# First batch of a sparse attention and feed-forward kernel: one score task for a pair of heads, over two accumulation banks, with the heads crosswise in the second

## The chip, the cores and the metric

The kernel runs on one core of a Trainium2 chip. The metric is the device time of one execution in microseconds (us): 869.84 us, the median of three runs (869.70 to 870.52). One more execution was taken with the hardware profiler; every duration below is from it.

The core has five engines with an instruction queue each, which run their queues in order. TensorE (PE) multiplies matrices into the banks of its accumulation memory; VectorE (DVE), ScalarE (ACT) and GpSimd (POOL) do elementwise work; SyncE (SP) issues transfers from memory. POOL does not read the accumulation banks here. An engine waits for another through semaphores.

## The reference

```python
def _attn_ref(q, k, v):
    scores = scale * np.matmul(q, k.transpose(0, 1, 3, 2))      # 8 batches, 8 heads, 576 x 576
    rel = pos[:, None] - pos[None, :]
    mask_local = (rel >= 0) & (rel < 32)
    mask_strided = (rel >= 0) & (pos[None, :] % 32 == pos[:, None] % 32)
    # heads 0 to 3 local, heads 4 to 7 strided
    scores = np.where(masks, scores, -1e9)
    attn = softmax(scores)                                       # (sum + 1e-9)
    return np.matmul(attn, v)

def _moe_ref(x, w_in, w_out):                                    # 4608 tokens, 512 -> 2048 -> 512
    h = x @ w_in
    g = np.maximum(h, 0.0) + np.log1p(np.exp(-np.abs(h)))
    return g @ w_out
```

## The kernel before, in words

Attention touches only a band of the scores: 32 queries see 64 keys. Heads go in pairs; a pair's 576 queries are 18 blocks of 32 queries by 64 keys, put as nine *chunks* of 128 rows by 64 columns: row 64 x place + 32 x head + lane, where place is 0 or 1. The feed-forward part takes chunks of 512 tokens: 16 steps `hidden` (twelve 128x512 products, line 819) and 16 steps `output` (twelve more, line 860) for each chunk. Each fp32 number is split into a high and a low part, so weights and activations need some preparation on ACT, DVE and POOL.

The batches after the first run their attention inside the dense stream of products, ordered by a planner. The change is about what stands before that stream: batch 0, four pairs n = 0 to 3 (0 and 2 local, 1 and 3 strided). Its order is a list written out by hand, `FIRST` (line 44): every name is a task, and each engine gets its instructions in that order. `ON_POOL`, `ON_VECTOR` and `WIDE` say which engine or which form a task takes. The names, n a pair and j a part of it:

- `q`, `k`, `v`, `wi`, `wo`: transfers, issued by SP; `W` and `W15` and the like: products on zeros that keep PE active.
- `S` scores (line 414). Before, a pair has two: part 0 has chunks 0 to 5, part 1 chunks 6 to 8 (`SPLIT`, line 25), each in a bank of its own, py[2 (n mod 2) + part]. The mask is added by products too: `ident_b` picks the rows (line 422). Pairs 0 and 2 use the same two banks, 1 and 3 the other two.
- `X` row maxima (line 575, DVE), `x` their negative as a bias (line 579, DVE or POOL), `E` exponentials (ACT). `E` takes one instruction with its accumulator for each chunk (line 585), or, for a part named in `WIDE`, one instruction for the whole part (line 567) after a subtraction `Y` on DVE (line 562), and then sums `Z` on DVE (line 571). `E` without `Y` reads the bank; with `Y`, the bank is free after `Y`.
- `r`, `R`, `M`: guard (622), reciprocal (626), normalization (630).
- `T` three transposes on PE (line 693) into one of two free banks, `C` the copy out of it (ACT or DVE), `V` the product with v (line 712).
- `H` and `L`: high and low part of the attention output for the feed-forward part (lines 753 and 751).
- `a`, `B`, `d`, `h`, `l` with `i` or `o` and a number: the five steps that prepare a block of weights.
- `Fa0`, `F0`, `Fa1`, `F3`, ...: `hidden` of chunk 0 (`Fa` the first three quarters of it); `O0`, ...: `output`. `D4` and `J4` are the q layout and the scores of the first pair of batch 1, `Y40` takes the mask and frees `J4`'s bank.

`late_scores` (line 457), for later batches, holds the same form of products as `S`: 64x32 weights, 64 columns. It writes two banks in turn, and puts the two heads crosswise in the second one.

Of the kernel before, what the change touches and what calls it, by code (L numbers as in the profile page):

```python
# [45 lines left out]
x10 r0 wi3 v2 E10 x11 E11 Bi0 R0 wi2 ao0 M0 W15 S20 X20 T01 S21 di0 x20 E20 v3 S30 wo1 S31 hi0 r1
T00 C01 ai1 Bo0 R1 X21 Y21 k4 q4 X30 wi4 X31 E21 li0 Y30 C00 T02 Z21 wi6 x31 M1 V00 do0 r2 C02 Bi1
E30 E31 T11 wi9 V02 R2 Z30 V01 H00 M2 C11 L00 wo2 T10 T12 H01 C10 C12 L01 T21 V10 r3 ai3 wo3 R3 M3
ho0 Bi3 V12 lo0 C21 V11 H10 L10 T22 H11 wi12 L11 T20 C20 wi8 C22 ai2 V21 V20 V22 T30 H20 T31 W23 W17
di1 C30 di3 wo6 L20 Bi2 H21 L21 di2 T32 hi3 hi2 V30 C31 C32 V31 hi1 ao1 V32 Bo1 Km li3 Fa0 H30 L30  # L50
H31 L31 D4 li2 v4 do1 J4 li1 Y40 ai4 F0 ho1 Bi4 ai6 A0 Ae0 q5 Fa1 F1 wi10 Al0 Y42 Y41 ai9 X4 di4 lo1
u0 s4 hi4 Gh0 wi14 A1 Bi9 E4 Bi6 Gl0 F3 Ae1 Al1 O0 di6 di9 hi6 ao3 u1 Kz Kl F2 li4 A3 wo15 ao2 k5
Bo3 wo13 Ae3 li6 ao6 wo4 wi5 hi9 Gh1 Al3 Gl1 li9 Z4 ai8 u3 Bi8 Bo6 r4 di8 F6 wi7 wo8 A2 Bo2 Ae2 do2
R4 Al2 O1 M4 do3 u2 W18 wo11 hi8 Gh3 ho3 ho2 Gh2 D5 Gl3 A6 Ae6 wo9 do6 ho6 wo5 Gl2 P43 lo2 wo7 F4
P40 P42 Al6 A4 ai5 Ae4 lo3 u6 Al4 ai7 P41 u4 li8 Bi7 q6 ai10 lo6 Gh4 Bi5 O2 Gh6 J5 di5 Y50 wo10 hi5
di7 ao4 li5 Bo4 O3 Y51 X5 hi7 li7 Bi10 s5 F5 do4 E5 wi11 ho4 di10 Gl4 v5 k6 Z5 F9 H41 Gl6 ao7 H40 A5
Bo7 ao5 Ae5 A9 Al5 lo4 r5 Bo5 ao9 R5 M5 do5 L40 wi15 Ae9 O4 u5 Al9 wo14 L41 do7 F7 ho5 Gh5 u9 ho7
P52 Gl5 lo5 A7 hi10 Ae7 P53 Gh9 P50 Al7 u7 F8 lo7 Gl9 ai12 wi13 D6 ai11 O5 P51 Gh7 Bo9 Bi11 di11 J6
Y60 O6 Bi12 do9 A8 Y62 Y61 hi11 li10 ho9 ao8 X6 Bo8 di12 s6 Ae8 hi12 E6 li11 F10 do8 Gl7 O7 Al8 li12
v6 Z6 u8 r6 ho8 A10 R6 M6 lo8 Gh8 ai13 Ae10 P61 Al10 Gl8 F11 A11 u10 k7 ao10 wo12 Bi13 Ae11 F12 di13  # L60
ai14 lo9 Gh10 W19 O8 hi13 ao11 Gl10 P62 Al11 H50 li13 ai15 P60 u11 A12 Bo10 F13 Ae12 Gh11 q7 k8 D7
O9 Bi14 H51 Bi15 Al12 Gl11 Bo11 di14 hi14 P63 A13 L51 Ae13 do10 L50 u12 Al13 u13 ho10 lo10 ao12 W21
do11 J7 ho11 di15 Bo12 Y71 H61 O10 H60 li14 hi15 li15 lo11 ao15 Gh13 do12 v7 Gh12 q8 F14 ho12 Y70
ao13 X7 Gl12 Gl13 Bo13 F15 s7 do13 E7 O11 A14 Z7 L60 r7 Ae14 ho13 Al14 R7 lo12 A15 u14 L61 M7 Ae15
# [1177 lines left out]
```

## Time and profile before

| | us |
|---|---|
| median of three runs | 869.84 |
| profiled execution, its own time | 871.17 |
| its span in the trace | 869.4 |
| PE busy in the span | 860.9 |
| DVE, ACT, POOL busy | 595.6, 411.6, 97.4 |

The span runs from the first to the last instruction of the program. PE busy counts every product from its start to its modelled end, so that 99% busy is not 99% of PE's peak; what helps the reader is where PE is not busy, and what it does where it is busy without doing dense products.

### The profile page before, as it was taken

What the parts mean: (1) busy time and instruction counts of PE and PEld (TensorE: products, weight loads), DVE (VectorE), ACT (ScalarE), POOL (GpSimd) and SP (SyncE); (2) the same over time, 40 slices, a digit from 0 to 9 for tenths busy, and PEclk for the clock granted to TensorE, in tenths of its full rate; (3) what the DMA queues carried; (4) which work ended last, traced back from release to release, by engine and by line L of the source; (5) the groups of instructions that cost most, each with busy time, mean ns of one, the idle gap of its engine ahead of it and who ended that gap; (6) DMA issues with size and microseconds to landing.
All of it is one profiled execution on the core that took longest, in us unless ns stands there. A gap on an engine that the chain in (4) does not pass through costs nothing.

```text
span 869.4 us, 15756 instructions
## 1 busy us (share of the span) xinstructions
PE 860.9 (99%) x6312; PEld 704.8 (81%) x6312; DVE 595.6 (69%) x1283; ACT 411.6 (47%) x730; POOL 97.4 (11%) x117
## 2 busy tenths in 40 slices
PE   8999999999999999999999999999999999999998
PEld 5788888888888888888888888888888888888886
DVE  4999968777777787777777787777877433333332
ACT  6887745444444454444544444435344343334333
POOL 4667532121200000000000000000000000000000
PEclk9999999999999999999999999999999999999999
DMA  9983112111301121011301131112100010001001
GB/s 320 377 309 124 43 29 89 44 56 30 104 29 37 34 85 48 15 56 29 104 29 56 29 104 29 35 35 81 54 15 16 1 48 1 1 1 49 1 1 48
DMA packets 46462, 56.41 MB, mean 65 GB/s; under 512 B 3322, under 2 KB 31670, under 8 KB 46390
## 3 DMA queue, kind: packets, MB, share of 16 engines
q1 hardware_dynamic: 46102, 55.09, 19.6%
q8 instruction: 49, 0.80, 0.4%
q10 hardware_dynamic: 288, 0.33, 0.1%
q14 instruction: 23, 0.19, 0.1%
HBM read 45.97 MB, written 9.44 MB: 64 GB/s over the span
## 4 chain that ended last, share of the span: by engine, by line
PE 98%; DVE 1%; ACT 1%; issue 0%; POOL 0%; DVEq 0%; ACTq 0%; POOLq 0%
PE py L860 45%; PE ph L819 45%; PE ps L538 1%; PE ph L485 1%; PE ps L524 1%; PE ph L469 1%; PE py L440 1%; PE pv L712 1%; PE idle L883 1%; PE ph L693 0%; PE po L524 0%; PE py L422 0%; PE po L538 0%; POOL w_o L295 0%; ACT x_h L753 0%
## 5 line engine op out<-in xcount | busy, mean ns | idle before, releaser
L860 PE MATMUL py<-w_o,gh 128*128 128x512 f32 x1152 | 358.0, 392 | 0.0
L819 PE MATMUL ph<-x_h,w_i 128*128 128x512 f32 x1152 | 355.4, 390 | 0.4 <-POOL w_o L295 0.2
L819 PEld LDWEIGHTS ph<-x_h,w_i 128*128 128x128 f32 x1152 | 215.7, 188 | 46.5 <-DVE u L840 1.0
L860 PEld LDWEIGHTS py<-w_o,gh 128*128 128x128 f32 x1152 | 214.1, 188 | 45.4
L831 ACT ACTIVATE u<-ph 128x512 f32<-128x512 f32 x144 | 86.2, 598 | 321.9 <-PE ph L819 321.9
L840 DVE SCALAR_TENSOR_TENSOR u<-ph,u 128x512 f32<-128x512 f32 x144 | 99.3, 689 | 191.1 <-ACT u L836 190.3
L860 PE MATMUL py<-w_o,gl 128*128 128x512 f32 x576 | 224.2, 389 | 0.0
L819 PE MATMUL ph<-x_l,w_i 128*128 128x512 f32 x576 | 224.1, 389 | 0.0
L860 PEld LDWEIGHTS py<-w_o,gl 128*128 128x128 f32 x576 | 108.1, 188 | 22.9
L819 PEld LDWEIGHTS ph<-x_l,w_i 128*128 128x128 f32 x576 | 108.1, 188 | 22.6
L836 ACT ACTIVATE u<-u 128x512 f32<-128x512 f32 x144 | 91.0, 632 | 4.3
L834 ACT ACTIVATE u<-u 128x512 f32<-128x512 f32 x144 | 91.0, 632 | 4.3
L853 DVE TENSOR_TENSOR gl<-u,gh 128x512 fp32r<-128x512 f32 x118 | 81.8, 695 | 9.8
L667 DVE STREAM_TRANSPOSE masks_pt<-kT_prob 32x128 f32<-32x128 f32 (+2 forms) x220 | 63.4, 288 | 2.8
L295 DVE CAST gh<-u 128x512 fp32r<-128x512 f32 x129 | 57.5, 446 | 10.0 <-DVE u L840 0.5
L614 ACT ACTIVATE kT_prob<-kT_prob 128x594 f32<-128x594 f32 (+2 forms) x28 | 22.1, 788 | 52.6 <-DVE kT_prob L608 52.6
L853 POOL TENSOR_TENSOR gl<-u,gh 128x512 fp32r<-128x512 f32 x26 | 35.7, 1374 | 76.7 <-DVE gh L295 66.2
L646 DVE STREAM_TRANSPOSE pt_groups<-kT_prob 32x160 f32<-32x160 f32 (+1 forms) x112 | 39.6, 354 | 3.1
L646 DVE STREAM_TRANSPOSE masks_pt<-kT_prob 32x160 f32<-32x160 f32 (+1 forms) x112 | 39.6, 353 | 3.0
L618 DVE TENSOR_REDUCE st<-kT_prob 128x11 f32<-128x594 f32 (+2 forms) x28 | 24.6, 879 | 20.5 <-ACT kT_prob L614 20.5
L295 ACT COPY qT<-kT_prob 128x576 f32<-128x576 f32 x28 | 35.7, 1275 | 2.3 <-DMA kT_prob<-in_qk_dram 1.3
L753 ACT CAST x_h<-ps 128x288 fp32r<-128x288 f32 (+5 forms) x34 | 12.0, 372 | 42.2 <-PE ps L524 22.3
(117 smaller groups left out, 603.9 us busy)
## 6 DMA issues: line engine op xcount, KB each, us to landing
kT_prob<-in_qk_dram SPq DMA_DIRECT2D x42, 288.0 KB, 3.8
out_dram<-o SPq DMA_DIRECT2D x35, 256.0 KB, 3.6
ri<-in_moe_w_in_dram SPq DMA_DIRECT2D x16, 512.0 KB, 7.3
ro<-in_moe_w_out_dram SPq DMA_DIRECT2D x16, 512.0 KB, 8.9
kT<-in_qk_dram SPq DMA_DIRECT2D x14, 288.0 KB, 6.6
v_in<-in_v_dram SPq DMA_DIRECT2D x14, 162.0 KB
v_in<-in_v_dram SPq DMA_DIRECT2D x14, 160.0 KB, 3.3
v_in<-in_v_dram SPq DMA_DIRECT2D x14, 128.0 KB, 3.1
```

The lines of the kernel that those rows point to most:

```text
L295: (engine.copy if engine is nc.scalar else engine.tensor_copy)(dst, src)
L614: nc.scalar.activation(pv, pv, AF.Exp, scale=SCALE)
L618: nc.vector.tensor_reduce(sm, pv, axis=AX.X, op=ALU.add)
L646: nc.vector.transpose(dst[:, :, :32], src[:, :, :32])
L667: nc.vector.transpose(pt_late[lo : lo + 32, h, first : first + src.shape[1], col : col + 32], src,)
L819: nc.tensor.matmul(ph, lhsT=w32["i", f][:, half, cc * P : (cc + 1) * P], rhs=x_of(x, cc)[:, t0 : t0 + n], start=(i == 0), stop=(i == 3 * N ...
L831: nc.scalar.activation(us[c, f], phs[c, f], AF.Abs)
L834: nc.scalar.activation(u, u, AF.Exp, scale=-1.0)
L836: nc.scalar.activation(u, u, AF.Ln, bias=1.0)
L840: nc.vector.scalar_tensor_tensor(u, in0=phs.pop((c, f)), scalar=0.0, in1=u, op0=ALU.max, op1=ALU.add)
L853: engine.tensor_tensor(g, us.pop((c, f)), ghs[c, f].bitcast(F32), op=ALU.subtract)
L860: nc.tensor.matmul(py[t], lhsT=g[:, sl], rhs=w32["o", f][:, half], start=(f == 0 and n == 0), stop=(f == NFC - 1 and n == 2),)
```

## The change

A pair's scores become one task `S{n}` that fills both of its banks. `SPLIT` is now five and four chunks. The chunks are issued in the order 0, 5, 1, 6, 2, 7, 3, 8, 4, so that the two banks take turns, and in the second bank head 0 stands in the rows of head 1 and the other way round. The masks are added by products of 64 rows by 32 columns of weights, one for each place and head (8 for a local pair, 12 for a strided one, where the second bank needs two pieces of the mask; before, 4 of 128 rows by 64 columns). For that the mask comes twice into a region of `qT`, once in each half of the partitions, by two transfers from ACT's queue; the old copy `mask_b` comes later by SP's queue (`mk`). A second identity `flip` with the halves exchanged, made by two copies on ACT, takes the transposed heads of the second bank back to their places.

`FIRST` and the three lists are written anew: part 0 of pair 0 and both parts of pair 3 are `WIDE` (before: part 1 of pair 2 and part 0 of pair 3), and other casts and copies are on other engines.

```diff
-SPLIT = [(0, 6), (6, 9)]
+SPLIT = [(0, 5), (5, 9)]
 FIRST = """
-mask k0 q0 k1 W S01 q1 wi0 S00 q2 k3 X01 x01 k2 X00 S11 E01 wo0 ai0 x00 S10 q3 wi1 E00 X11 X10 v0 v1
+mask q0 W k0 S0 X00 X01 x01 wi0 q1 ai0 Y00 Bi0 E00 k1 di0 E01 k2 q2 S1 X11 wo0 Z00 x11 X10 S2 r0 R0
...
 WIDE = """
-21 30
+00 31 30
...
+    mask_early = qT[:, : 6 * 64].bitcast(BF16)
...
+    flip = room[2][:, 2 * NTILE * D + P : 2 * NTILE * D + 2 * P]
+    for h in range(2):
+        nc.scalar.copy(
+            flip.rearrange("p (a h c) -> p a h c", a=2, h=2)[:, :, h],
+            ident_b.rearrange("p (a h c) -> p a h c", a=2, h=2)[:, :, 1 - h],
+        )
...
+    def mask_pieces(n, part):
+        lo, hi = SPLIT[part]
         if is_local(n):
-            return mask_b[:, : 6 * 64] if part == 0 else mask_b[:, 64 : 4 * 64]
-        return mask_b[:, 6 * 64 :] if part == 0 else mask_b[:, 6 * 64 : 9 * 64]
+            return [(lo, hi, part, None)]
+        if part == 0:
+            return [(lo, hi, 6, 0)]
+        return [(lo, 6, 6 + lo, 0), (6, hi, 6, 1)]
...
-            for place in range(2):
-                nc.tensor.matmul(
-                    ps[rows[place], : 64 * (hi - lo)],
-                    lhsT=ident_b[:, rows[place if is_local(n) else part]],
-                    rhs=mask_of(n, part),
...
+            for part in range(2):
+                pieces = mask_pieces(n, part)
+                for lo, hi, chunk, sort in pieces:
+                    for place in range(2):
+                        for h in range(2):
+                            to = 64 * place + 32 * (h if part == 0 else 1 - h)
+                            head = slice(64 * h, 64 * h + 64)
+                            one = 64 * h + 32 * (place if sort is None else sort)
+                            at = 64 * (lo - SPLIT[part][0])
+                            nc.tensor.matmul(
+                                ps[part][to : to + 32, at : at + 64 * (hi - lo)],
+                                lhsT=ident_b[head, one : one + 32],
+                                rhs=mask_early[head, 64 * chunk : 64 * (chunk + hi - lo)],
...
-        for x in range(lo, hi):
+        for x in (0, 5, 1, 6, 2, 7, 3, 8, 4):
...
-                ident,
+                ident if 3 * i + t < SPLIT[0][1] else flip,
...
-    first["mask"] = lambda: nc.scalar.dma_start(mask_b, masks)
+        rows = masks.rearrange("(b a l) c -> a b l c", a=2, b=2)
+        for h in range(2):
+            nc.scalar.dma_start(mask_early[64 * h : 64 * h + 64], rows[h])
+    first["mk"] = lambda: nc.sync.dma_start(mask_b, masks)
...
+            task(f"S{n}", scores, n)
             for j in range(2):
-                task(f"S{n}{j}", scores, n, j)
```

On PE, pair 2 stood as follows before: `S20` (bank py_107), then one transpose task of pair 0, then `S21` (bank py_108).

```order
L422 MATMUL py_107<-masks_pt,ident_b 64x384
L422 LDWEIGHTS ident_b
L422 MATMUL py_107<-masks_pt,ident_b 64x384
L440 MATMUL py_107<-early_h_97,raw_q_201 32x64 x24
L693 MATMUL ph_111<-room_116,early_l_94 128x4x32 x3
L422 LDWEIGHTS ident_b
L422 MATMUL py_108<-masks_pt,ident_b 64x192
L422 LDWEIGHTS ident_b
L422 MATMUL py_108<-masks_pt,ident_b 64x192
L440 MATMUL py_108<-early_h_97,raw_q_201 32x64 x12
```

And now, from the last of its mask products to the transposes of pair 0 that follow:

```order
L441 MATMUL py_108<-qT,ident_b 32x256
L461 MATMUL py_107<-early_h_97,raw_q_223 32x64 x4
L461 MATMUL py_108<-early_h_97,raw_q_223 32x64 x4
L461 MATMUL py_107<-early_h_97,raw_q_223 32x64 x4
L461 MATMUL py_108<-early_h_97,raw_q_223 32x64 x4
L461 MATMUL py_107<-early_h_97,raw_q_223 32x64 x4
L461 MATMUL py_108<-early_h_97,raw_q_223 32x64 x4
L461 MATMUL py_107<-early_h_97,raw_q_223 32x64 x4
L461 MATMUL py_108<-early_h_97,raw_q_223 32x64 x4
L461 MATMUL py_107<-early_h_97,raw_q_223 32x64 x4
L714 MATMUL ph_111<-room_116,early_l_94 128x4x32 x3
L714 MATMUL ph_112<-room_116,early_l_94 128x4x32 x3
```

The banks take turns, pair 2 stands whole before the first transposes, and two transpose tasks of pair 0 stand ahead of pair 3, with the third.

ACT's queue began like this before (early_l_94, 96, 98 and 100 hold pairs 0 to 3):

```order
L915 DMA masks_pt<-in_masks_dram 128x768
L241 CAST room_116<-ident_b 128x128
L585 ACTIVATE early_l_94,st_204<-py_108,st_204 128x64 x3
L779 ACTIVATE a_i_228<-ri_173 128x512
L585 ACTIVATE early_l_94,st_204<-py_107,st_204 128x64 x6
L585 ACTIVATE early_l_96,st_267<-py_109,st_267 128x64 x6
L585 ACTIVATE early_l_96,st_267<-py_110,st_267 128x64 x3
```

And so now:

```order
L942 DMA qT<-in_masks_dram 64x1x768
L241 CAST room_116<-ident_b 128x128
L244 CAST room_116<-ident_b 128x2x32 x2
L942 DMA qT<-in_masks_dram 64x1x768
L800 ACTIVATE a_i_211<-ri_207 128x512
L588 ACTIVATE early_l_94<-early_l_94 128x5x64
L606 ACTIVATE early_l_94,st_203<-py_108,st_203 128x64 x4
L606 ACTIVATE early_l_96,st_273<-py_110,st_273 128x64 x4
L606 ACTIVATE early_l_96,st_273<-py_109,st_273 128x64 x5
L800 ACTIVATE a_o_346<-ro_275 128x512
L301 COPY masks_pt<-ph_111 128x4x96
L606 ACTIVATE early_l_98,st_343<-py_107,st_343 128x64 x5
```

Pair 0 has four single exponentials in place of nine, the second half of the mask is issued after three casts, and a copy `C00` of pair 0 (the row with masks_pt) stands behind the exponentials of pair 1.

SP's queue before, from its first transfer:

```order
L304 DMA early_h_93<-in_qk_dram 128x576
L292 DMA raw_q_144<-in_qk_dram 128x576
L304 DMA early_h_95<-in_qk_dram 128x576
L292 DMA raw_q_171<-in_qk_dram 128x576
L759 DMA ri_173<-in_moe_w_in_dram 128x4x128
L292 DMA raw_q_201<-in_qk_dram 128x576
L304 DMA early_h_99<-in_qk_dram 128x576
L304 DMA early_h_97<-in_qk_dram 128x576
```

And now:

```order
L298 DMA raw_q_146<-in_qk_dram 128x576
L310 DMA early_h_93<-in_qk_dram 128x576
L780 DMA ri_207<-in_moe_w_in_dram 128x4x128
L298 DMA raw_q_209<-in_qk_dram 128x576
L310 DMA early_h_95<-in_qk_dram 128x576
L310 DMA early_h_97<-in_qk_dram 128x576
L298 DMA raw_q_223<-in_qk_dram 128x576
```

early_h_93, 95, 97 and 99 are k of pairs 0 to 3, raw_q their q; the first block of weights (ri) has moved ahead of both transfers of pair 1.

## Rows read from the trace of the kernel before

**Rows 1.** Busy time of each engine in five stretches, from the end of the first products on zeros on (120 to 140 and the last 9.4 us are left out); the columns are the stretch, then busy us (and instructions) of PE, weight loads, DVE, ACT and POOL, the granted TensorE clock, the share of the DMA engines and GB/s.

```profile
5.56:17.57 12.01, 10.01 (x310) 7.37 (x309) 6.59 (x17) 9.27 (x52) 4.28 (x8) 0.86 1.04 361
17.57:29.46 11.89, 10.70 (x141) 8.11 (x134) 9.81 (x26) 9.36 (x27) 6.26 (x13) 1.00 1.07 378
29.46:34.00 4.54, 4.22 (x86) 2.98 (x85) 4.54 (x9) 3.28 (x6) 2.13 (x2) 1.00 1.06 397
34.00:120.00 86.00, 86.00 (x740) 70.66 (x744) 82.56 (x176) 65.78 (x115) 54.02 (x50) 1.00 0.48 160
...
140.00:860.00 720.00, 720.00 (x4922) 594.14 (x4921) 477.59 (x1031) 309.57 (x508) 20.65 (x15) 1.00 0.13 39
```

**Rows 2.** The same view, cut where the clock changes.

```profile
10.08:13.80 3.72, 1.72 (x55) 1.30 (x55) 2.34 (x7) 3.72 (x28) 0.67 (x2) 1.00 1.05 383
13.80:16.80 3.00, 3.00 (x79) 2.15 (x78) 2.18 (x7) 3.00 (x18) 2.35 (x3) 0.50 1.12 358
16.80:20.60 3.80, 3.51 (x62) 2.66 (x61) 3.26 (x10) 3.04 (x12) 1.61 (x3) 0.95 1.06 334
```

**Rows 3.** The chain of waits from 5 to 35 us, in order of time: start, us, what. Its pieces follow each other, so that each is a step and not a duration with its tail.

```profile
7.70 0.37 PE py L422 x4
8.07 0.55 PE py L440 x24
8.62 0.28 PE py L422 x2
8.91 0.92 PE py L440 x48
...
13.30 0.52 PE ph L693 x3
...
14.11 0.80 PE py L440 x24
14.91 0.46 PE py L422 x2
15.37 1.44 PE py L440 x48
...
23.62 0.80 PE ph L693 x6
...
24.45 1.53 PE pv L712 x24
...
29.53 2.12 PE ph L819 x9
```

**Rows 4.** PE in order of time (start, us, line, operation, the tiles, count, and in brackets the idle time before it and what ended it): the first mask products of pair 2, the first and the last of the 72 score products of `J4`, what follows them, and `Fa1` at 34.00.

```profile
11.76 0.35 PE L422 MATMUL py<-masks_pt,ident_b 128*64 128x384 bf16 x2 [1.68 <-ACT early_l L585]
...
31.91 0.26 PE L506 MATMUL ps<-kT_prob,qT 64*32 64x64 f32 x4
...
32.49 0.41 PE L506 MATMUL ph<-kT_prob,qT 64*32 64x64 f32 x13
32.82 0.74 PE L819 MATMUL ph<-x_h,w_i 128*128 128x512 f32 x2
...
34.00 0.70 PE L819 MATMUL ph<-x_h,w_i 128*128 128x512 f32 x2 [0.20 <-POOL w_o L295]
```

**Rows 5.** ACT in order of time: the cast of the identity, the first two exponentials of `E00`, the weight step `ao0`, and a whole-part exponential of 384 columns.

```profile
2.02 0.30 ACT L241 CAST room<-ident_b 128x128 f32<-128x128 bf16 x1
...
9.83 0.31 ACT L585 ACTIVATE early_l<-py,st 128x64 f32<-128x64 f32 x1
...
10.12 0.31 ACT L585 ACTIVATE early_l<-py,st 128x64 f32<-128x64 f32 x1
...
14.17 0.77 ACT L779 ACTIVATE a_o<-ro 128x512 f32<-128x512 f32 x1
...
18.90 0.54 ACT L567 ACTIVATE early_l<-early_l 128x384 f32<-128x384 f32 x1
```

**Rows 6.** DVE in order of time: maxima and subtraction of 384 columns, sums of 192, the last normalization of batch 0 (pair 3), and `Y40`.

```profile
16.88 0.56 DVE L575 TENSOR_REDUCE st<-py 128x6 f32<-128x384 f32 x1 [0.52 <-PE py L440]
...
18.00 0.55 DVE L562 TENSOR_TENSOR early_l<-py,st 128x384 f32<-128x384 f32 x1
18.46 0.34 DVE L571 TENSOR_REDUCE st<-early_l 128x3 f32<-128x192 f32 x1
...
22.33 0.76 DVE L630 TENSOR_TENSOR early_l<-early_l,st 128x576 f32<-128x576 f32 x1
...
33.38 0.48 DVE L597 TENSOR_TENSOR kT_prob<-ph,masks_pt 128x320 f32<-128x320 f32 x1
```

**Rows 7.** SP's transfers in order of time (start, us, line, tiles): the first block of w_out, and those of v of pair 0 and the second one of pair 1.

```profile
4.58 0.43 SPq L765 DMA_DIRECT2D ro<-in_moe_w_out_dram  x1
...
7.92 0.34 SPq L344 DMA_DIRECT2D room<-in_v_dram  x1
9.24 0.38 SPq L351 DMA_DIRECT2D room<-in_v_dram  x1
...
10.92 0.43 SPq L351 DMA_DIRECT2D room<-in_v_dram  x1
```

**Rows 8.** The waits of SP's queue: who waited for what, us in total, times, longest.

```profile
SPq L344 <- DMA raw_q<-in_qk_dram: 1.7, 2, 1.4
...
SPq L351 <- DMA ri<-in_moe_w_in_dram: 1.0, 1, 1.0
```

More of the change, by code (lines that the diff above doesn't have):

```diff
@@ L44 @@
 FIRST = """
-mask k0 q0 k1 W S01 q1 wi0 S00 q2 k3 X01 x01 k2 X00 S11 E01 wo0 ai0 x00 S10 q3 wi1 E00 X11 X10 v0 v1
[L46 to L64, printed above, removed]
@@ L65 @@
-ao14 P70 O12 D8 P72 lo13 Al15 P73 Gh14 P71 Bo14 O13 u15 J8 k9 do14 H71 Gl14 Gh15 ho14 L71 H70 Qa0
-lo14 q9 L70 Q0 Bo15 do15 ho15 QA0 Gl15 v8 Qu0 lo15 O14 Q1 Qh0 QA1 Ob15 Qu1 O15 y3 y1 y2 Qh1 y0 Ql1
-Ql0
+mask q0 W k0 S0 X00 X01 x01 wi0 q1 ai0 Y00 Bi0 E00 k1 di0 E01 k2 q2 S1 X11 wo0 Z00 x11 X10 S2 r0 R0
+x10 M0 T00 E11 hi0 li0 E10 X21 X20 ao0 q3 C00 k3 T01 v0 Bo0 x20 E20 x21 T02 r1 S3 do0 C01 C02 R1 X30
+M1 X31 Y30 E21 Y31 wi1 T10 E31 E30 V02 r2 v1 R2 ai1 wi3 V01 V00 T11 v2 H00 C10 Z30 T12 Z31 L00 Bi1
@@ new lines @@
+C11 W8 H01 M2 wi2 W10 r3 L01 T20 C12 ho0 ai3 C20 V10 q4 T21 V12 C21 di1 v3 R3 V11 hi1 wi4 H10 T22 M3
+L10 H11 mk L11 Bi3 T31 C22 C31 W1 k4 ai2 V21 V22 di3 V20 Bi2 H20 T32 L20 li1 hi3 H21 C32 wo1 li3 T30
+W4 wi6 L21 C30 wi9 V32 V31 lo0 V30 D4 di2 H31 L31 H30 ai4 Fa0 L30 J4 wo3 hi2 ao1 F0 wo6 Bi4 W22 wo5
+k5 di4 wo2 li2 A0 Ae0 Y40 wi8 hi4 wi10 Bo1 Al0 do1 q5 Y41 Y42 wo4 u0 Fa1 wi15 F1 ai6 Gh0 X4 ho1 ai9
+A1 lo1 v4 Ae1 Bi6 wi5 Gl0 s4 di6 li4 F3 O0 W21 ao6 Bi9 wi14 wi7 Al1 hi6 E4 A3 u1 di9 Gh1 F2 Kz Ae3
@@ L72 @@
 """.split()
 ON_VECTOR = """
-M0 C01 C10 M3 ho0 hi2 li2 li1 Gl0 li4 li6 Gh1 li9 li5 Gl4 Gl6 M6 lo9 lo10 lo11 Gl12 Gl13 lo12 ho14
-Gl15 lo15
+M0 li0 C01 C02 C10 hi1 M3 lo0 li2 hi4 lo1 Gl0 li6 li9 Gl4 lo4 Gl6 li12 li15 Gh12 Gl12 ho12 Gl13 lo11
+lo12 Gl15 ho15
 """.split()
@@ L409, in mask_of, with scores @@
             return mask_g.unsqueeze(1).broadcast_to([P, hi - lo, GROUP])
+    def mask_pieces(n, part):
+        lo, hi = SPLIT[part]
         if is_local(n):
[L411 to L428 removed]
+            return [(lo, hi, part, None)]
+        if part == 0:
+            return [(lo, hi, 6, 0)]
+        return [(lo, 6, 6 + lo, 0), (6, hi, 6, 1)]
+    def scores(n):
+        ps = [py[2 * (n % 2) + part] for part in range(2)]
+        pss[n, 0], pss[n, 1] = ps
+        def add(first):
+            for part in range(2):
[11 more added lines that the diff above has]
+                                rhs=mask_early[head, 64 * chunk : 64 * (chunk + hi - lo)],
+                                start=first and lo == SPLIT[part][0],
+                                stop=not first and hi == SPLIT[part][1],
+                            )
         if n > 0:
             add(True)
[L433 removed]
+        for x in (0, 5, 1, 6, 2, 7, 3, 8, 4):
+            part = 0 if x < SPLIT[0][1] else 1
+            lo, hi = SPLIT[part]
             for place in range(2):
```

29 lines of the change are left out of this document (19 added, 10 removed).

## The prediction, made before the changed kernel was run

> **What bounds the kernel now.** I read first the busy time by stretches [rows 1]: from 34 to 120 us and from 140 to 860 PE is busy for the whole of it, at the full clock, with dense products. Nothing the change does to batch 0 can shorten that. What it can move is the time at which the dense stream begins; one microsecond there is one microsecond at the end, as long as the other engines keep up (DVE is 96% busy from 34 to 120, 82.56 of 86). [...] The chain of waits [rows 3] then says what PE does: scores and masks until about 17.6, transposes and products with v, and the first dense products at 29.53. PE in order of time [rows 4] shows the one long wait: 1.68 us, ending at 11.76, when `S20` needs the bank that the six exponentials of `E00` are reading; and `Fa1` at 34.00. There the view names a cast on POOL; but the bank it writes was `J4`'s, and comes free with `Y40`, which runs from 33.38 to 33.86 [rows 6]. I take `Y40` as the releaser.
>
> My reference is `Fa1`: 34.00 in the profiled execution. It took 871.17 us, 1.33 over the median of 869.84; I subtract what moves there from the median.
>
> **The scores.** 72 score pieces of a pair took 0.55 + 0.92 = 1.47 us at the full clock (`S11`, `S10`), and 0.80 + 1.44 = 2.24 at the lower one (`S21`, `S30`) [rows 3]. `J4` has 72 of the same form, over two banks crosswise, from 31.91 to 32.82: 0.91 us [rows 4]. So the crossing should give back 0.55 us a pair, 2.2 us for four. The bounds are 1.47 (no gain) and 0.6 (the first 60 of `J4`'s came in 0.58 us, 31.91 to 32.49); I take 0.9, the nearest row, and 1.4 at the lower clock.
>
> **The masks.** Four products of 384 and 192 columns took 0.37 us [rows 3]; now there are 8 of 320 and 256, or 12. If all four places of a bank run at once, 0.37 or less; if the two halves of the array follow each other, twice that, 0.74, and for 12 some 1.1. I take 0.6. [...] By the higher price only `S3`'s counts on the way to `Fa1`, some 0.4 us.
>
> So PE's own work falls by 0.3 to 0.6 us a pair. But scores of pairs 0 and 1 stand ahead of waits, so that I follow the queue instead.
>
> **The new order, step by step** (steps between starts: an exponential 0.29, a whole part 0.45 [rows 5]; maxima or subtraction of 320 columns 0.40, of 256 0.35, from 0.46 for 384 (18.00 to 18.46), a normalization 0.7 [rows 6]; transposes 0.42 a task, products with v 0.5 [rows 3]).
>
> 1. `S0` starts at 5.6, when the products on zeros end; that hasn't changed. Its scores last to 7.0, its masks to 7.6. The second half of the mask is issued after the cast at 2.02 [rows 5] and two more, at about 2.7 and not at 0.8. The former mask had landed by 4.58, since w_out's first block waited for its place in the queue [rows 7]: under 3.8 us. So it lands by 6.5, and `S0`'s masks hide it; if not, all of pair 0 moves.
> 2. DVE: `X00`, `X01`, `x01`, `Y00` to 8.8. ACT: `E00` as one instruction, then four exponentials of `E01` to 10.5 (before: 11.7).
> 3. `S1` now waits for its transfers. SP keeps some transfers out and issues another when an old one has landed; so v at 7.92 and 9.24 shows when q of pair 1 and the first weights had [rows 7, 8]. `S1` needs the same six that had landed by 9.24, and in the new order k of pair 1 is the last of them. PE is idle from about 8.2 to 9.2; behind it wait `S2` and all transposes. `S1` ends at 10.1. `S2` needs two more, which by the same measure are there at 10.9; it ends at 11.8 (before: 14.9).
> 4. DVE gives `M0` by 12.3; `T00` starts at 12.4, not 13.30. `T02` needs a bank that `C00` on ACT frees, and `C00` stands behind nine exponentials of pair 1 and `ao0` (step 0.57): 14.6. Behind `T02` stands `S3`: it ends at 16.7 at the full clock, at 17.55 at the lower one.
> 5. DVE's two maxima and two subtractions of pair 3, ACT's two whole-part exponentials, DVE's sums and eight small pieces lead to `M3`, done at 23.05, or 23.9. Before: 23.09 [rows 6]. So the last softmax is no earlier.
> 6. What is gained is that less is left: after `M3`, PE had five transpose tasks and six products with v until 29.5; now three and six. 3 x 0.42 + 6 x 0.5 = 4.3, some 0.6 for copies and casts on ACT between them: `Fa0` at 27.9, or 28.75.
> 7. `Fa0` 2.1, `J4` 0.91; `Y40` follows at once (DVE has finished its `L` tasks by then) with 0.48; `Fa1` at 31.95, or 32.8.
>
> So `Fa1` comes 2.05 us earlier with the full clock, 1.2 with the lower one in `S3`. I have counted no handoffs, which are 0.02 to 0.15 us each, some ten in the chain (0.14 from the end of `Y40` at 33.86 to 34.00): about 0.4 less where nothing hides them. Expected: 0.8 to 1.65 us, and 1.1 as the forecast, for the lower clock is what the row of `S3` shows now. 869.84 - 1.1 = 868.7.
>
> **After 34 us.** DVE's list from `L30` to the end of chunk 0 loses six `l`, a normalization, a `gh` and a cast and gains four `l`, a `gh` and three casts: some 1 us less, started earlier by as much as PE is. The second copy of the mask adds 0.2 MB to transfers that run at 378 GB/s [rows 1]: 0.5 us, on blocks of weights that are needed some us after landing. I count nothing for both; if the cover fails, it is the second rival.
>
> **Rivals.**
>
> *The full clock all the way.* If the shorter waits keep the clock up, `Fa1` gains 1.65 to 2.05: 867.8 to 868.2. For it: the wait of 1.68 us is gone. Against it: the new idle stretches are 8.2 to 9.2, 11.8 to 12.4, 13.3 to 14.7 and about 17 to 17.8, so that PE is busy for half of 10 to 14 us again, as in the first of rows 2. If also handoffs and copies run tighter than I have it (ACT's copies of pair 3), 867.
>
> *The gain is given back in the dense stream.* DVE at 96% or a block of weights sets the pace between 34 and 120 us, and PE waits there for what it won: 869.3 to 870.2. For it: DVE's share. Against it: no wait at all in 86 us now, and the prepared work starts earlier too.
>
> *The low clock stays: slower.* Now PE works without a break from 13.8 to 16.8, and the next 3.8 us have 0.95 [rows 2]. In the new order it waits once more before the transposes of pair 1, for `M1` on POOL (to 17.8). If the clock stays low through the products of pairs 0 and 1 (17.8 to 23: six transpose tasks and six products with v, 2.5 + 3.0 us at the full clock), each further stretch as long as that of rows 2 (3.0 us at 0.50) costs half of itself, 1.5. With one `Fa1` comes at 32.8 + 1.5 = 34.3, 870.1; with two at 35.8, 871.6; with the handoffs of 0.4 on top, 872.0. It decides from the first on. For it: four breaks in place of two. Against it: with twice the duration the same work leaves no breaks, which is what ended the low stretch now; and products on zeros (`W8`, `W10`, `W1`, `W4`) stand in the gaps.
>
> *The crossing doesn't shorten the scores* (they stay at 1.47, and the masks cost 1.1): `S2` and `S3` end 0.5 and 1.0 later, `Fa1` gains 0 to 0.4, 869.5 to 869.8. `J4`'s 0.91 speaks against it.
>
> **How the numbers follow.** Forecast (868.2 to 869.1) 0.47; full clock 0.24; given back or no shorter scores, together 0.15; the low clock stays 0.14, half of it with two stretches or with another delay on top. What a measurement of this kernel can tell from no change is about 0.2%, or 1.74 us: faster is under 868.1, slower over 871.6. The full clock gives most of the chance of faster, and a chain tighter than mine a little more: 0.29. Slower is the low clock with two stretches, and what I have not thought of: 0.11. The same: 0.60. The range: down to 866.9 for the full clock with a tight chain, up to 871.2 for one low stretch more with handoffs on top; the forecast alone has 868.2 to 869.1.
>
> **What would show it.** In the changed profile: 72 pieces of a pair's scores in about 0.9 us at the full clock; `S1` starting at about 9.2 after a wait for a transfer; `M3` ending close to 23 us; only three transpose tasks behind it; `Fa0` near 28 and `Fa1` near 32.5; a clock of 0.50 somewhere between 13 and 18 us and nowhere after 21; PE busy all of 34 to 120. I am wrong if `Fa1` comes after 33.5 or before 31.5, if the clock is low after 21 us, or if PE has more than 0.5 us of idle time between 34 and 120.

## The result: slower, and the profile after

The changed kernel takes 876.22 us (median of four runs, 875.57 to 877.31), beside 870.18 for the kernel before: a ratio of 1.0067, with a 95% interval of 1.0049 to 1.0085. The forecast of 868.7 and its range up to 871.2 are missed by 5 us and more. The profiled execution took 875.57 us at a mean granted clock of 1.000, 4.40 more than that of before (at 0.998).

First the busy time by stretches, as in [rows 1]:

```profile
5.56:17.57 12.01, 4.70 (x213) 3.44 (x212) 3.83 (x12) 2.82 (x14) 0.46 (x2) 1.00 0.84 261
17.57:29.46 11.89, 9.66 (x212) 7.47 (x199) 10.68 (x28) 10.64 (x48) 4.93 (x7) 1.00 1.08 365
...
34.00:120.00 86.00, 85.89 (x710) 70.29 (x706) 81.30 (x175) 70.74 (x123) 51.38 (x53) 1.00 0.54 180
...
140.00:860.00 720.00, 720.00 (x4922) 594.14 (x4922) 479.64 (x1036) 309.33 (x508) 23.50 (x20) 1.00 0.13 40
```

The dense stretches are as good as full, as before. The loss stands in the first: PE is busy for 4.70 of 12 us (10.01 before), and the transfers too are slower, 261 GB/s in place of 361. PE's waits (who waited for what, us in total, times, longest) and PE in order of time name the place:

```profile
PE py L441 <- DMA qT<-in_masks_dram: 4.2, 1, 4.2
PE py L461 <- DMA early_h<-in_qk_dram: 1.8, 1, 1.8
PE ph L714 <- POOL early_l L651: 1.5, 1, 1.5
PE py L441 <- ACT early_l L606: 1.2, 1, 1.2
```

```profile
7.44 1.35 PE L461 MATMUL py<-early_h,raw_q 64*32 64x64 f32 x72 [1.81 <-DMA early_h<-in_qk_dram]
8.49 0.47 PE L441 MATMUL py<-qT,ident_b 64*32 64x320 bf16 x1
13.18 0.72 PE L441 MATMUL py<-qT,ident_b 64*32 64x320 bf16 x19 [4.22 <-DMA qT<-in_masks_dram]
13.76 1.34 PE L461 MATMUL py<-early_h,raw_q 64*32 64x64 f32 x72
...
21.28 0.32 PE L441 MATMUL py<-qT,ident_b 64*32 64x320 bf16 x12
21.41 1.03 PE L461 MATMUL py<-early_h,raw_q 64*32 64x64 f32 x72
...
34.13 0.73 PE L840 MATMUL ph<-x_h,w_i 128*128 128x512 f32 x2
...
38.13 0.62 PE L840 MATMUL ph<-x_h,w_i 128*128 128x512 f32 x2
```

`S0` starts at 7.44, not at 5.6, because its keys are late; its masks start at 8.49 and then stop, with 4.22 us of idle time up to 13.18. `Fa0` comes at 34.13 (29.5 before) and `Fa1`, the last row, at 38.13 (34.00): 4.13 of the 4.40 us. The chain of waits gives the culprit a length, in its first piece (start, us, what):

```profile
2.00 11.14 DMA qT<-in_masks_dram
13.18 0.47 PE py L441 x3
```

The second of the two mask transfers, 98 KB (64 rows of 1536 bytes), takes 11.14 us from its issue to its landing. ACT's queue is q10 in the table of queues (packets, MB, share of 16 engines' time). Before, between 2 and 4 us and between 4 and 8:

```profile
q10 hardware_dynamic: 143, 0.20, 29.5%
...
q10 hardware_dynamic: 1, 0.00, 0.0%
```

After, from 2 to 4, 4 to 8, 8 to 12, and 12 to 13.2 us:

```profile
q10 hardware_dynamic: 19, 0.03, 5.3%
...
q10 hardware_dynamic: 57, 0.08, 7.7%
...
q10 hardware_dynamic: 52, 0.08, 7.0%
...
q10 hardware_dynamic: 4, 0.00, 1.1%
```

The same 0.2 MB were through by 4 us; now they come at 0.02 MB a us for nine us, and take 7 to 8% of the engines' time, little more than one engine of sixteen. The packets also hint at how many engines take part. Of the 144 before, 128 are the mask's 128 rows and 16 are left over; of the 132 now, 4 are left over. If what is left over counts the engines of a transfer, one packet each, that is 16 engines for the one before, and two for each of the two now. This is an estimate from the counts; the trace doesn't name the engines.

### The profile page after: what moved, and what is told of

It reads as the page before. It is cut to its first block, busy times and chain, and to the rows that moved or that the text cites. A ratio compares the mean times of both kernels' runs of the same rounds, so it can differ in the third digit from the quotient of the medians.

```text
span 873.8 us, 15821 instructions
## 1 busy us (share of the span) xinstructions
PE 858.7 (98%) x6338; PEld 703.6 (81%) x6338; DVE 596.1 (68%) x1289; ACT 412.2 (47%) x724; POOL 92.8 (11%) x111
## 4 chain that ended last, share of the span: by engine, by line
PE 96%; DMA 1%; ACT 1%; DVE 1%; issue 0%; POOL 0%; DVEq 0%; ACTq 0%
PE py L881 45%; PE ph L840 45%; DMA qT<-in_masks_dram 1%; PE ps L559 1%; PE ph L506 1%; PE ps L545 1%; PE ph L490 1%; PE pv L733 1%; ACT early_l L606 0%; PE po L545 0%; PE ph L714 0%; PE po L559 0%; PE pv L913 0%; PE ph L527 0%; DVE st L596 0%
## 5 line engine op out<-in xcount | busy, mean ns | idle before, releaser
L667 DVE STREAM_TRANSPOSE pt_groups<-kT_prob 32x192 f32<-32x192 f32 (+1 forms) x112 | 39.6, 354 | 3.8 <-POOL kT_prob L651 0.8
```

The lines of the kernel that those rows point to most:

```text
L667: nc.vector.transpose(dst[:, :, :32], src[:, :, :32])
```

## The experiments

Theory 1 was that the shape of the transfers does it. The source is `masks.rearrange("(b a l) c -> a b l c")[h]`, whose outermost dimension is 2, and by the estimate above each of the two transfers runs on two engines; the theory takes the shape for the cause. The share of 7 to 8% of sixteen engines agrees with few engines; the runs below decide. Rivals: the mask is late because its second half is issued late, behind casts; or the new order is slower by itself.

All fourteen runs, with the ratio to the kernel before on the same chip, and the mean granted clock over each kernel's runs:

| run | median us (runs) | ratio, 95% interval | clock |
|---|---|---|---|
| four | 870.92 (11) | 1.0005, 0.9996 to 1.0013 | 0.9952 |
| one | 871.46 (12) | 1.0006, 0.9996 to 1.0017 | 0.9958 |
| before_two | 877.01 (5) | 1.0071, 1.0058 to 1.0084 | 0.9966 |
| one_seq | 870.63 (11) | 1.0005, 0.9994 to 1.0016 | 0.9969 |
| pad60 | 871.39 (10) | 1.0016, 1.0007 to 1.0026 | 0.9945 |
| pad140 | 872.60 (6) | 1.0026, 1.0014 to 1.0038 | 0.9925 |
| hold | 873.04 (5) | 1.0035, 1.0022 to 1.0048 | 0.9952 |
| flipb | 872.21 (8) | 1.0022, 1.0012 to 1.0033 | 0.9960 |
| hold1 | 872.26 (11) | 1.0018, 1.0009 to 1.0027 | 0.9955 |
| hold2 | 873.33 (6) | 1.0030, 1.0019 to 1.0042 | 0.9972 |
| relief | 871.03 (11) | 1.0008, 0.9999 to 1.0018 | 0.9957 |
| relief_seq | 870.70 (11) | 1.0004, 0.9995 to 1.0013 | 0.9969 |
| relief_w | 870.94 (11) | 1.0001, 0.9993 to 1.0010 | 0.9978 |
| four_w | 872.33 (11) | 1.0016, 1.0007 to 1.0025 | 0.9972 |

The kernel before had a median of 870.16 to 870.68 beside them, at a mean clock of 0.9983 to 0.9989.

### The transfer of the mask: four, one, before_two

```diff
-        rows = masks.rearrange("(b a l) c -> a b l c", a=2, b=2)
         for h in range(2):
-            nc.scalar.dma_start(mask_early[64 * h : 64 * h + 64], rows[h])
+            for b in range(2):
+                to, of_ = 64 * h + 32 * b, 64 * b + 32 * h
+                nc.scalar.dma_start(mask_early[to : to + 32], masks[of_ : of_ + 32])
```

> The changed kernel with its early mask loaded by four transfers of 32 rows each, in place of two whose source has an outermost dimension of two. Theory (the two transfers are served by two of the 16 DMA engines each, and 98 KB on one engine take until 13 us): PE's wait for the mask before S0's products falls from 4.2 us to under 0.5, S1's queries and k are no longer late either, Fa1 starts at 32 to 33.5 us and the time is 867.5 to 869.5. Rival 'issued late' (the second half goes out behind the casts, and several transfers are queued): three of the four go out behind the casts here, so the wait stays at 2 us or more and the time above 873. Rival 'the order itself' (the new order is slower even with its mask in time): no long wait for the mask, and still 870.5 or more.

For `one` the loop is a single `nc.scalar.dma_start(mask_early, masks_early)`, from an added input with its rows in the wanted order.

> The changed kernel with its early mask loaded by one transfer of 128 rows, issued at once, from an extra input that holds the same mask with its rows already in the order that the products want. Both the theory of the two DMA engines and the rival 'issued late' expect 867.5 to 869.5, Fa1 at 32 to 33.5 us and no wait for the mask; the rival 'the order itself' expects 870.5 or more. Against the run with four transfers it tells what is left of the issuing: by the theory of the engines the two are within 0.5 us.

For `before_two`, on the kernel before:

```diff
-    first["mask"] = lambda: nc.scalar.dma_start(mask_b, masks)
+        for h in range(2):
+            rows = masks[64 * h : 64 * h + 32]
+            rows = bass.AP(tensor=rows.tensor, offset=rows.offset, ap=[[0, 2], rows.ap[0], rows.ap[1]])
+            nc.scalar.dma_start(mask_b[64 * h : 64 * h + 64], rows)
```

> The kernel before, with its mask loaded by two transfers whose source has an outermost dimension of two (the 32 rows read twice, so that the bytes and the rows written are the same), the second behind the cast as in the changed kernel; nothing else is changed. Its first two copies of 32 rows are the same rows, so what it masks is not the reference's. Theory of the two DMA engines: the mask lands at 8 to 13 us in place of under 4.6, S01 waits for it on PE, and the time is 872 to 876. Rival 'issued late': at most 1.5 us more than the kernel before, under 871.5. Rival 'the order itself': no difference to the kernel before (869.5 to 870.5).

Measured: 5.3 us come back with `four` (876.22 to 870.92), though the last of its four transfers is issued at 2.29 us, later than the second one of the changed kernel (2.00), and 4.8 with `one`. In `four`, ACT's queue has 192 packets for the mask, 64 more than it has rows: by the same estimate, 16 engines for each of the four. The shape alone, put into the kernel before, costs it 6.2 us (1.0071; 877.01 is a little over the 872 to 876 expected). Its first mask products, in the kernel before and in `before_two`:

```profile
6.36 0.37 PE L422 MATMUL py<-masks_pt,ident_b 128*64 128x192 bf16 x2
...
12.00 0.37 PE L422 MATMUL py<-masks_pt,ident_b 128*64 128x192 bf16 x2 [5.11 <-DMA early_h<-in_qk_dram]
```

The view puts this wait down to a transfer of keys, but these products read the mask and the identity alone, and 51 of the 132 packets of the mask's queue come between 8 and 12 us, none from 12.0 to 13.2. PE's waits and first rows in `four`, with its first stretch:

```profile
PE py L461 <- issue: 1.8, 1, 1.8
PE py L441 <- ACT early_l L606: 1.4, 1, 1.4
...
PE ph L714 <- POOL early_l L651: 0.7, 1, 0.7
...
PE py L441 <- DMA qT<-in_masks_dram: 0.3, 1, 0.3
```

```profile
5.56 1.35 PE L461 MATMUL py<-early_h,raw_q 64*32 64x64 f32 x72
...
11.02 0.89 PE L461 MATMUL py<-early_h,raw_q 64*32 64x64 f32 x39
13.71 0.69 PE L461 MATMUL py<-early_h,raw_q 64*32 64x64 f32 x33 [1.80 <-issue]
```

```profile
5.56:17.57 12.01, 8.06 (x320) 6.16 (x321) 8.55 (x22) 7.95 (x43) 1.88 (x5) 0.72 1.08 375
```

`S0` starts at 5.56 again, and the transfers run at 375 GB/s: the keys were late only because of the mask's transfers. That these sat on engines which also carry a part of everything else would explain it, but is not shown: the trace doesn't name the engines. So the shape of the transfers is shown as the cause, and "issued late" falls. But the time is that of the kernel before, not the 867.5 to 869.5 expected; it is what the rival "the order itself" had expected (870.5 or more). Something else holds the new order, and the rows show a new break: `S2` stops after 39 of 72 pieces for 1.80 us, put down to "issue", which is nothing the profile names.

### Turns between the banks: one_seq

On `one`, `for x in (0, 5, 1, 6, 2, 7, 3, 8, 4)` becomes `for x in range(NCHK)`.

> The kernel with one transfer for the early mask, and the chunks of a pair's scores one after the other (0 to 8), so that the two banks don't take turns; the rows are still crosswise. If taking turns between banks is what shortens the scores, 72 pieces take about 1.4 us at the full clock again in place of about 0.8, Fa1 comes 0.5 to 1 us later than with turns, and so does the end. If the pieces are short because of something else, scores and time are those of the kernel with turns, within 0.3 us.

`S2`'s first 40 pieces, in `one` and in `one_seq`:

```profile
10.16 0.71 PE L462 MATMUL py<-early_h,raw_q 64*32 64x64 f32 x40
...
10.66 0.83 PE L462 MATMUL py<-early_h,raw_q 64*32 64x64 f32 x40
```

They take 0.83 us from first start to last end in place of 0.71. All 72 of `S1`, from their start to the next mask product, take 0.90 in place of 0.77. So turns shorten a pair's scores by 0.1 us or a little more, not by the half microsecond from 1.4 that was expected; what else makes them shorter than the 1.47 us of before stays open. The end is not later without turns (870.63 and 871.46, with intervals of the ratio that overlap). `S2` breaks after 40 pieces here as well (2.94 us; 4.12 in `one`), though the piece behind it is of another chunk (5, and 7 in `one`). So the break seems to hang on the place in the program and not on an operand.

### The break in S2: pad60, pad140, flipb

Theory 2, "code": PE's instructions come by a queue of their own, and the next ones weren't there. The table of queues of `four` has, over the whole span, and from 11 to 12 us:

```profile
q8 instruction: 50, 0.82, 0.4%
...
q8 instruction: 1, 0.02, 6.0%
```

50 packets of 16 KB for PE's 12,676 products and weight loads: some 254 a packet. The first packet within the span starts at 11.25 us and ends at 12.20; PE goes on at 13.71. How much PE had done by then is counted by the view of busy time (PE's and the weight loads' instructions in brackets):

```profile
0.00:11.95 11.95, 8.57 (x221) 4.44 (x222) 4.40 (x13) 5.00 (x20) 4.61 (x23) 0.94 0.88 308
11.95:13.70 1.75, 0.00 (x0) 0.00 (x0) 1.40 (x3) 1.75 (x14) 0.11 (x1) 0.50 1.11 359
```

221 and 222. `pad60` and `pad140` put more instructions ahead of S0, at the same columns: the 10 products on zeros of 512 columns become 40 of 128, or 80 of 64. In `flipb` the mask comes as before, and a bf16 identity with its halves swapped does the crossing, so that there are fewer mask products (against `four`; not all lines are shown):

```diff
-                nc.scalar.dma_start(mask_early[to : to + 32], masks[of_ : of_ + 32])
+    first["mask"] = lambda: nc.scalar.dma_start(mask_b, masks)
...
+                                ps[part][64 * place : 64 * place + 64, at : at + 64 * (hi - lo)],
+                                lhsT=(ident_b, flip_b)[part][:, one : one + 64],
+                                rhs=mask_b[:, 64 * chunk : 64 * (chunk + hi - lo)],
```

> The kernel with four mask transfers, with 60 more instructions on PE ahead of S0: the 10 products on zeros of 512 columns are 40 of 128. Nothing else is changed. Theory 'code' (PE has its first instructions at hand, and goes on only when the next packet of queue 8, 16 KB, has come): the break that stands after 39 of S2's 72 pieces comes 60 instructions earlier in the program, after some 10 of them, and the packet starts up to 1 us earlier than 11.3 us. Rival 'operand' (the piece behind the break waits for a transfer that the views don't name): the break stays at piece 39 or 40. Time: 870 to 872 by both, since a break of 1.5 to 3 us stays in S2.

> The same with 140 more instructions on PE ahead of S0 (80 products of 64 columns on zeros). Theory 'code': the break moves into S1, some 300 products and weight loads into the program as it was, so after about 40 to 50 of S1's 72 pieces; the packet starts at about 9.5 to 11 us, S1 ends at 11.5 to 13 in place of 9.4, and the time is 871 to 874, for the whole chain of S1 moves. Rival 'operand': no break inside S1, the break in S2 stays, 870 to 872.

> The changed kernel with the mask as in the kernel before: one transfer of 128 rows in the old layout, and products of 64 columns out, of which those for the second bank take an identity with its halves swapped. Scores, crossing and order are the changed kernel's; it has 4 or 6 mask products a pair in place of 8 or 12, that is 44 instructions fewer in the three pairs up to S2's end. Theory 'code': the break in S2 begins 24 to 32 instructions later in the program (those of S0 and S1 that are gone), after some 50 to 56 of its 72 pieces, and is shorter by some 0.2 to 0.5 us only: 869.5 to 871. Rival 'operand': break at piece 39 or 40. Against the changed kernel both expect 5 us less, since the mask lands by 5 us.

| run | break after | products + loads ahead | first packet, us | break, us | PE goes on |
|---|---|---|---|---|---|
| four | S2, piece 39 | 221 + 222 | 11.25 to 12.20 | 1.80 | 13.71 |
| one | S2, 40 | 222 + 222 | 12.76 to 13.68 | 4.12 | 14.99 |
| pad60 | S2, 9 | 221 + 222 | 9.37 to 10.42 | 0.50 | 11.91 |
| pad140 | S1, 50 | 222 + 222 | 8.41 to 9.52 | 1.60 | 10.95 |
| flipb | S2, 54 | 222 + 222 | 12.02 to 12.98 | 2.91 | 14.34 |

The break moves through the program as expected (9 for some 10, 50 for 40 to 50, 54 for 50 to 56) and always follows the same count, 443 or 444; PE goes on 1.3 to 1.5 us after the packet has ended. Theory 2 holds, and "operand" falls. The rows of `pad60` that count it, to be read beside those of `four`:

```profile
0.00:11.45 11.45, 7.50 (x221) 6.51 (x222) 3.86 (x11) 4.46 (x16) 4.12 (x22) 1.00 0.87 306
11.45:11.90 0.45, 0.00 (x0) 0.00 (x0) 0.45 (x3) 0.45 (x5) 0.41 (x1) 0.81 0.98 331
```

What missed is when the packet comes: 9.37 in `pad60` (10.3 or later expected, and a break of 1.5 to 3 us), 8.41 in `pad140` (9.5 to 11), and later than in `four` in `flipb`, whose time missed as well (872.21, expected 869.5 to 871). I had no measure for it. The kernel before has its packet at 11.63 to 12.57 and has issued 221 + 221 by 14.05, which is 1.48 us after the packet: by this reading it stood at the same edge, just late enough to show no break.

### Less data ahead of the packet: hold, hold1, hold2, relief

When is the packet asked for? If PE does so each time it has used up one packet's worth (443 less 254, its 189th instruction: an estimate from these counts), it starts between 2.0 us later (`hold1`, 7.12 to 9.17) and 6.2 (`one`, 6.55 to 12.76). The sixteen engines are nearly full then (a share of 0.88 up to 11.95, 1.11 behind it, in the rows of `four`). In the next runs SP is held by a transfer of one row that has to wait for a score task. `hold`, `hold1` and `hold2` also bring all queries and keys forward, and v and the weights' edits back; `relief` keeps the order of `four` and only adds, in `FIRST`, `hold` ahead of `wo0` and `hold2` ahead of `wi1`:

```diff
+    first["hold"] = lambda: nc.sync.dma_start(raws[0][0:1, :], qk[order[0][0], order[0][1], 0:1, 0])
+    first["hold2"] = lambda: nc.sync.dma_start(raws[2][0:1, :], qk[order[2][0], order[2][1], 0:1, 0])
```

> The kernel with four mask transfers, with fewer bytes on the way when PE needs its next instructions: the queries and keys of all four pairs are loaded first, then SP waits for the end of S1 (a transfer of one row does the waiting), and only then come v and the first two blocks of weights, whose casts and subtractions stand some places later. Theory 'code' (the packet stands behind the data that was issued before it): the packet starts by 9.5 us and not at 11.3 to 12.8, no break inside S2 over 0.5 us, S2 ends by 13 us in place of 14.3, Fa1 at 32 to 33 us, 868 to 870, unless the weights come too late for Fa0 (then up to 872). Rival 'operand': S2 without a break too, since its operands are there early, but the packet still starts at 11 us or later. Rival 'the order itself': as slow as with four transfers, 870.5 to 871.5, though the break is gone.

> As the kernel in which SP waits for the end of S1, but the edits of the first block of weights stand where they stop neither ACT nor DVE (cast behind C00, the rest behind x21 and M1), and that block is loaded ahead of v. One wait of SP. Theory 'code': the first packet of queue 8 starts by 9.5 us, S2 ends by 12.2, S3 by 15; then SP has again issued all it can, so that the second packet starts 3 to 5 us after PE has passed its 449th instruction (11.5), at 14.5 to 16.5, and no instruction behind the 705th, the transposes of T10, starts before 17 us. 868.5 to 871. Rival 'POOL': T10 starts when M1 is done, at 16 to 16.5, whatever the packet does.

> The same with a second wait of SP, for the end of S2, ahead of v of pair 0 and all that follows. Theory 'code': the second packet too starts within 3 us of PE's passing its 449th instruction, so by 14.5, T10 starts at 16 to 17 as soon as M1 is done, Fa0 at 27 to 28.5 and Fa1 at 31 to 32.5, which are the times of the prediction: 867.5 to 869.5. It can be lost again where v or the weights now come too late (a wait for a transfer at V00 or Fa0 would show it), or where the clock is low in the longer breaks. Rival 'the order itself' (the chain behind S3 bounds Fa0 in the new order, not PE's start): 870 to 871 with both packets in time.

> The kernel with four mask transfers and its order of work as it is; SP alone is held back at two places, so that less data stands ahead of PE's next packet of instructions, without DMA running dry: before the first block of w_out it waits for the end of S0 (some 7.5 us, with transfers on the way that last to 9.7), and before the second block of w_in for the end of S2. Theory 'code': the first packet starts by 9.8 us (11.25 without the waits), the break in S2 is under 0.5 us (1.8), S2 ends by 13 (14.3); the second packet starts by 15 (16.56), T10 by 18.2 (18.77); Fa1 at 32.2 to 33.2, 869.3 to 870.5, some 0.5 to 1 us less than with four transfers alone. Rival 'the order itself' (M1, M2 and M3 on DVE and POOL bound the way to Fa0, so that an earlier S2 wins nothing): packets and S2 as above, but T10 at 18.7 or later and 870.7 to 871.5. Rival 'it isn't the queue': the packets start as late as before, 11 us and 16.5.

The packet starts at 9.09, 9.17 and 9.06 in the first three, the break shrinks to 0.72 in `hold` and 0.25 in `hold2` (in `hold1`, none of 0.2 or more is listed), and `S2` ends by 12.0 to 12.3: that is the prediction's 11.8, at last. They are slower all the same (872.26 to 873.33, where 867.5 to 871 was expected), and the traces show waits that I brought in myself: in `hold`, DVE waits 2.9 us for the cast of the first weights, which I had put too early for its transfer, and `T10` then 4.7 us for `M1`; in `hold2` the second packet too is in time (13.03; `T10` starts at 17.56, as `M1` ends), and then a copy on DVE waits behind the edits of weights that came late (2.2 us). So these show the packet's part, but not what the order could do: the rival "the order itself" is neither shown nor excluded.

`hold1` shows a second edge. Its second packet ends at 17.58. PE, in order of time, at `T10`:

```profile
17.78 0.48 PE L715 MATMUL ph<-room,early_l 128*128 128x128 f32 x1 [2.35 <-POOL early_l L652]
19.05 0.58 PE L715 MATMUL ph<-room,early_l 128*128 128x128 f32 x2 [0.80 <-issue]
```

`M1` frees one transpose, and the next two wait for code: 348 + 349 instructions stand ahead, some 253 more than at the first edge. (The expectations put the two edges at the 449th and the 705th instruction; the traces record 443 or 444 and 697 products and loads ahead of them.) `pad60` has the same edge at the same count, inside `S3`, 1.44 us after its second packet ends (16.22):

```profile
17.66 0.68 PE L461 MATMUL py<-early_h,raw_q 64*32 64x64 f32 x29 [0.75 <-issue]
```

`relief` is the cleanest, though only half a success. Its packets start at 10.96 (9.8 expected) and 14.58, and the break is 1.43 (under 0.5 expected). The profiled run of it took 869.57 us, with `Fa0` at 28.40 and `Fa1` at 32.41, 1.59 earlier than before. That is 1.60 less than the profiled run of before, but only 0.6 less than what the kernel before takes on the same chip at a clock of 1.000 (870.20, the mean of four runs). And the median of its eleven runs is 871.03 (869.3 to 870.5 expected): the profiled run is the only one with a clock of 1.000, the others have 0.994 to 0.996. Two rows of the stretch view, from 10 to 14 and 14 to 17.57 us, first of that run of `relief`, then of `four` (the number after POOL's is the clock):

```profile
10.00:14.00 4.00, 1.46 (x78) 1.27 (x78) 3.65 (x10) 3.73 (x27) 0.87 (x2) 1.00 0.80 277
14.00:17.57 3.57, 2.30 (x93) 1.75 (x91) 3.57 (x11) 3.32 (x20) 1.67 (x3) 1.00 0.56 165
```

```profile
10.00:14.00 4.00, 1.29 (x68) 1.07 (x75) 3.35 (x9) 3.72 (x25) 0.87 (x2) 0.56 1.07 374
14.00:17.57 3.57, 3.57 (x107) 2.74 (x92) 3.03 (x8) 2.77 (x15) 1.01 (x3) 0.54 1.12 359
```

The two stretches hold much the same work, not quite the same (93 and 107 products): it takes 2.30 us of PE at a mean clock of 1.00, and fills 3.57 at one of 0.54. The nine transposes of pair 0 alone take 0.88 + 0.55 us of PE in `relief` and 2.37 in `four`.

### Turns again, and the clock: relief_seq, four_w, relief_w

> The same with the chunks of a pair's scores one after the other, so that the two banks don't take turns. If taking turns shortens the scores and S3 is on the way to Fa0, S3's 72 pieces take 1.4 to 1.5 us at the full clock in place of 0.8 to 1.0, and the end comes 0.3 to 1.0 us later than with turns; if PE's own time there is hidden behind maxima, exponentials and the packets of instructions, the two are within 0.3 us.

870.70 beside 871.03: 0.3 us less, and not 0.3 to 1.0 more. That fits PE's own time in the scores being hidden behind maxima, exponentials and code. The profiled run of `relief_seq` had the lower clock in `S3`, so it doesn't show the 1.4 to 1.5 us at the full clock; `S1` took 0.89 us at it, and 0.79 in `relief`.

`four_w` and `relief_w` add two products on zeros ahead of `S1` and four ahead of `S2`, in waits of PE:

```diff
+    first["Wa"] = lambda: dummies(2)
+    first["Wb"] = lambda: dummies(4)
```

> The kernel with SP held back at two places, with two products on zeros ahead of S1 and four ahead of S2, where PE waits for a transfer and for ACT. Theory 'clock' (what is left of the loss is the longer stretch at the lower clock, which these waits bring on): mean granted clock 0.998 or more in most runs (0.9957 without the products), and a median of 869.3 to 870.2, 0.8 to 1.5 us less than without them. Rival 'the breaks in the code': the clock falls all the same behind the break in S2, mean 0.995 to 0.997, and 870.7 to 871.5. Rival 'not the clock': 0.998 or more and still 870.7 or more.

> The kernel with four mask transfers with the same six products on zeros, and SP free. Theory 'clock': mean granted clock 0.998 or more (0.9952 without), 869.5 to 870.5, though the break in S2 stays at some 1.8 us. Rival 'the breaks in the code': 0.995 to 0.997 and 870.7 to 871.3. Twelve instructions more ahead of S2 put the break some 6 pieces earlier, after 33 of 72.

The clock rises, to 0.9978 and 0.9972, and the times don't fall: 870.94 and 872.33. The products are instructions too. The break comes after 33 pieces of `S2`, as expected, and lasts longer, 1.91 and 2.63 us in place of 1.43 and 1.80. Three runs of `relief_w` at a clock of 1.000 took 870.5 on average, as the kernel before does (870.4, eight runs). So the clock alone is not what is left. How the rest splits between the clock, the wait for code and the order itself stays open: products that keep the clock up also use up the code at hand. No version beat the kernel before.

## Why the prediction was wrong, step by step

**Step 1 is the one that failed**: "So it lands by 6.5, and `S0`'s masks hide it; if not, all of pair 0 moves." I took 3.8 us, the landing of one transfer of 128 rows, for a new transfer of half the bytes, and never asked what its shape does to it. The second half was issued at 2.00, earlier than the 2.7 that I reckoned, and landed at 13.14, and all of pair 0 moved. I had named what it would cost, but gave it no rival and no price. What the runs showed in its place: two transfers that took 7 to 8% of the sixteen engines' time and came in over 11 us, and a price of 5.3 us by `four` and 6.2 by `before_two`.

**Step 3** has a second fault, which step 1 hid. "`S2` needs two more, which by the same measure are there at 10.9; it ends at 11.8": in `four` its scores do start at 11.02, and end at 14.3, as PE has no code after 221 products and 222 weight loads. The wait of 1.68 us ahead of `S20` [rows 4] isn't gone, as the rival of the full clock has it, but shorter and earlier (1.37 us, to 10.91, in `four`); and what it gives back could by this reading be won only up to that edge: the 222nd product of before came at 14.05, 1.48 us after its packet. The page of before showed q8 with its 49 packets; I read past that line.

**Steps 2, 4, 5 and 6** come close where the mask is in time. `T10` waits for `M1` "to 17.8": it starts at 18.77 in `four`, 18.19 in `relief`, 17.56 in `hold2`. `M3`, with 23.05 or 23.9 forecast, ends at 24.27 in `four` and 23.39 in `relief`. `Fa0` (27.9 or 28.75) is at 29.48 in `four` and 28.40 in `relief`, `Fa1` (31.95 or 32.8) at 33.48 and 32.41. **Step 7** leaves out a term: `Fa0`, `J4` and `Y40` as it names them add up to 3.5 us, and 4.05 stands there. The 4.05 is right (4.00 in `four`, 4.01 in `relief`), since the three products of `F0` stand between `J4` and `Fa1` (32.67 to 33.48 in `four`) and outlast `Y40`. **Scores and masks** were priced a little too high: 0.9 us for 72 pieces, and 0.83 from `S0`'s start to its first mask product at the full clock in `relief` (5.57 to 6.40); 0.6 for the masks, where the 12 of `S3` hold the scores up by 0.13 (21.28 to 21.41 above). The higher price (0.74, and some 1.1 for 12) is not borne out: both halves of the rows wrote each bank, and the 12 products still cost less than the 0.37 us of four products before. The rival "the crossing doesn't shorten the scores" was wrong in its number, for they fell from 1.47; but the turns between the banks account for 0.1 of it only (0.71 us for 40 pieces, and 0.83 without turns).

**The rival of the low clock** was right in kind: with the mask mended, the mean clock is 0.9952 in place of 0.9987, and three of the changed kernel's own four runs had 0.989 to 0.991. Of the versions that neither move the weights' edits nor add products, five runs had 1.000 (of `one`, `one_seq`, `relief` and `relief_seq`): they took 869.14 to 870.69 us, 869.6 on average, where the kernel before took 870.3 at 1.000 on the same two chips (17 runs). So the new order with its mask in time seems worth some 0.6 us at the full clock, and most of its runs didn't have that clock. My forecast of 868.7 is 2.2 us under `four`'s 870.92. Of these, 0.8 is the reference: the kernel before took 869.84 in the three runs that I started from, and 870.62 beside `four`. Code and clock have a part in the other 1.4; no run splits it.

**"After 34 us"** held: 0.11 us of PE idle from 34 to 120.

## What to carry to other kernels

Before pricing a moved transfer by an old one, look at its shape: two transfers from a rearranged source, its outermost dimension 2, kept `S0`'s masks waiting for 4.22 us here and brought other transfers late with them, and the same bytes in four transfers of whole row blocks for 0.29 (`four`). Where many small products stand at a program's start beside saturated transfers (a share of 0.88 and more here), count PE's instructions (products and weight loads) and look at when the instruction queue's packets come: an idle stretch named "issue" that stayed at 443 or 444 of them when the program was moved was code that hadn't arrived, and a wait taken away ahead of it won nothing beyond that point. Products on zeros against a low clock are instructions as well: six of them moved the break from piece 39 to 33.
